# A fused attention and feed-forward kernel: who takes the first statistics, where the scaled rows come from, and how one-column matmuls are mixed with query heads

## The chip, the cores and the metric

The kernel runs on one core of a Trainium2 chip. Time is device microseconds of that core for one execution; the lower, the better. "PE" is the matmul engine (TensorE), "DVE" VectorE, "ACT" ScalarE, "SP" the engine that issues most loads. Each timed execution also reports the mean granted clock of PE as a share of full speed (1.000 is full).

## The reference, cut to what matters

```python
mod = (silu(c) @ w_mod)                        # c: 1 x 1024, w_mod: 1024 x 6144
sa, ca, ga, sb, cb, gb = ...                   # six vectors of 1024
h = layernorm(x) * (1 + ca) + sa               # x: 2048 x 1024
x = x + ga * attention(h)                      # 32 query heads of 128, 4 kv heads, last 512 keys
h = layernorm(x) * (1 + cb) + sb
x = x + gb * ffn(h)                            # 1024 -> 3584 -> 1024
```

All inputs are bf16. The attention part computes `q = h @ wq` for each of 32 heads and each of 4 blocks of 512 rows of x.

## The kernel before

Only the first phase changes. It brings in the first 512 rows of x (four tiles of 128 rows), normalises and transposes them, and computes the first seven query heads. Afterwards a long, regular sequence of steps begins (scores, exponentials, next query head, outputs). The first score matmul, written `s_ps` in the profile, marks its start; the first output matmul, `o_ps`, comes 4.34 us later in an undisturbed execution.

The trick of the first phase is this: `h = n * (1 + ca) + sa`, with `n` the normalised rows. The scaled part `hs = n * ca1` (`ca1` is `1 + ca`) can go into the query matmuls as soon as a few columns of `ca1` are known, and the part of `sa` enters as a bias per head, `bias_q = wq^T sa`. Both `ca1` and `sa` come from matmuls whose right side is a single column (`mod_cols`), and `bias_q` too (`shift_cols`).

```python
def stats_0(t):                                 # mean and variance of one tile on DVE, then
    mv = ln[t] = ...                            # 1/sqrt on ACT
    ln_stats(t, mv)
    rstd_0(t)
def act_sum(t): ...                             # the same statistics on ACT: sum, then
def act_squares(t): ...                         # squared differences (two passes)

stats_0(0); act_sum(3); stats_0(1)
xpose_0(0, ln_norm(0)); warm(4)                 # xpose_0: PE transposes into h0_ps, warm: filler matmuls
act_squares(3); stats_0(2); rstd_0(3, 1.0 / D)
xpose_0(1, ln_norm(1)); warm(4)
n2 = ln_norm(2); n3 = ln_norm(3)
mod_cols(1, 0, ca1, True, (0,))                 # first 128 values of ca1
xpose_0(2, n2); xpose_0(3, n3)
mod_cols(1, 0, ca1, True, (1, 2, 3))
# h0_ps: two PSUM tiles of [128, 4, 512] bf16; row group dt lies in h0_ps[dt // 4][:, dt % 4]
nc.scalar.activation(out=hs[0][:, 0, :], in_=h0_ps[0][:, 0, :], func=ACT.Identity, scale=ca1[:, 0:1])
nc.vector.tensor_copy(out=h10[:, 0:2, :], in_=h0_ps[0][:, 0:2, :])
h_scale(1)                                      # DVE: hs row 1 from the SBUF copy h10
nc.vector.tensor_copy(out=h10[:, 2:4, :], in_=h0_ps[0][:, 2:4, :])
h_scale(2); h_scale(3)
nc.scalar.copy(out=h10[:, 4:8, :], in_=h0_ps[1])
# ... cut ...
for dt in range(4):                             # "rounds": heads 4, 5, 6 with hs row dt
    for g in range(4, H0):
        q0(g, (dt,))
for i in range(2):                              # heads 0 to 3; their PSUM is the PSUM of h0_ps
    t = big("q_ps")
    ...
    if i == 0:
        mod_cols(1, 1, ca1, True)               # second half of ca1
# ... cut: heads 0 to 3 with rows 4 to 7 ...
sa_cols(0)                                      # 32 one-column matmuls: first half of sa
q0(4, range(4, DT))                             # 4 matmuls of 512 columns
# ... cut ...
shift_cols(0)                                   # 28 one-column matmuls: first half of bias_q
sa_cols(1)
q0(5, range(4, DT))
shift_cols(1)
q0(6, range(4, DT))
for g in range(4):
    put_q(g, q0_ps[g], bias_q[:, g:g + 1], g % 2 == 1)   # heads 0, 2 on DVE, 1, 3 on ACT
```

Nearly all loads of this phase stand in one queue, in this order: four tiles of x, then the `w_mod` blocks for `ca1` and `sa` and the first `wq` blocks in turns, then k (transposing loads), then v (four), then the `wq` blocks of heads 8 to 11.

## Time and profile before

| before | value |
|---|---|
| time | 1274.93 us, median of 3 (1273.68 to 1275.57) |
| span of the profiled execution, granted clock | 1271.9 us, 1.000 |
| first `hs` row scaled | 11.15 us |
| `mod_cols(1,1)` starts on PE | 17.17 us |
| `sa_cols(0)` starts on PE | 23.15 us |
| `bias_q` complete (starts) | 28.45 us |
| first `s_ps`, first `o_ps` | 30.24, 34.58 us |

From the profile's page of before, its first line of busy time by engine and the chain of work that ended last by engine:

```profile
PE 1262.7 (99%) x7587; PEld 641.2 (50%) x7587; DVE 609.0 (48%) x1335; ACT 334.9 (26%) x439; POOL 1.3 (0%) x10
...
PE 98%; DVE 1%; DMA 0%; issue 0%; ACT 0%; ACTq 0%
```

PE is busy nearly all the time, and it is the chain. Of the 9.2 us that PE does not fill, 3.8 lie in the first 30 us and 5.2 in the last 6 (from 1266 us, where the last outputs are stored, which the change does not touch); in between there are 0.2. So a change in the first phase can gain only what it takes off the start of the regular steps.

The next lines are from the timeline of before: start in us, duration in us, engine, source line, operation, output and inputs, shapes, number of instructions, and in brackets how long the engine sat idle first and what ended that.

```profile
9.65 1.00 DVE L852 TENSOR_SCALAR xn<-x,mv 128x1024 bf16<-128x1024 bf16 x2 [0.95 <-ACT mv L954]
...
11.15 0.69 ACT L996 ACTIVATE hs<-h_ps,modT 128x512 bf16<-128x512 bf16 x1 [1.11 <-PE h_ps L948]
...
12.03 0.69 DVE L998 COPY hT<-h_ps 128x1024 bf16<-128x1024 bf16 x1
12.76 0.35 DVE L993 TENSOR_SCALAR hs<-hT,modT 128x512 bf16<-128x512 bf16 x1
...
13.16 0.81 PE L1013 MATMUL q_ps<-hs,wq 128*128 128x512 bf16 x3 [0.47 <-DVE hs L993]
...
14.15 3.18 PE L1013 MATMUL q_ps<-hs,wq 128*128 128x512 bf16 x14 [0.18 <-DVE hs L993]
...
17.17 0.94 PE L773 MATMUL mod_ps<-siluc,wm 128*128 128x1 bf16 x32
...
23.15 0.94 PE L773 MATMUL mod_ps<-siluc,wm 128*128 128x1 bf16 x32
...
25.91 0.94 PE L773 MATMUL mod_ps<-siluc,wm 128*128 128x1 bf16 x32 [0.26 <-DVE bias_q L1027]
...
28.45 0.17 DVE L1029 TENSOR_TENSOR bias_q<-sh_ps,bias_q 128x7 f32<-128x7 f32 x1 [1.20 <-PE sh_ps L1024]
...
30.24 0.59 PE L1153 MATMUL s_ps<-qT,kT 128*128 128x512 bf16 x2
```

Three waits can be read here. DVE waits 0.95 us for ACT's statistics before the last two normalisations. PE waits 0.47 us for `hs` row 1, because DVE first copies 1024 elements a partition out of PSUM (0.69) and scales the copy after that. PE waits 0.26 us for `bias_q` before the second `sa_cols`.

### The profile page before, as it was taken

The numbers are of one execution on the slowest core, as the hardware profiler recorded it, in microseconds if no ns is written. First come the engines' busy times: TensorE is split into PE (matmuls) and PEld (weight loads), VectorE is DVE, ScalarE is ACT, GpSimd is POOL, SyncE is SP. The second block draws the span as 40 slices with busy tenths as digits, with TensorE's granted clock in tenths as the row PEclk, the third lists the DMA queues.
The fourth block names the chain that finished last, engine by engine and source line by source line (L and its number), as shares of the span: only waits on it lengthen the run. The fifth ranks groups of instructions, "written<-read, shape, count | busy, mean of one in ns | idle before, by whom it ended". The sixth has DMA issues, their size and how long they took to land.

```text
span 1271.9 us, 18166 instructions
## 1 busy us (share of the span) xinstructions
PE 1262.7 (99%) x7587; PEld 641.2 (50%) x7587; DVE 609.0 (48%) x1335; ACT 334.9 (26%) x439; POOL 1.3 (0%) x10
## 2 busy tenths in 40 slices
PE   8999999999999999999999999999999999999998
PEld 4555555555555555555554444444444444444444
DVE  4766568977587756476664632311222112221122
ACT  3543334443343433334341111011100111011100
POOL 0000000000000000000000000000000000000000
PEclk9999999999999999999999999999999999999999
DMA  9897657768556655455575466536633565425701
GB/s 290 203 246 180 175 133 176 170 171 195 142 134 173 152 137 153 113 154 112 120 203 145 135 224 184 161 96 212 210 116 102 171 213 179 157 91 172 242 22 64
DMA packets 306844, 204.46 MB, mean 161 GB/s; under 512 B 145601, under 2 KB 303297, under 8 KB 306754
## 3 DMA queue, kind: packets, MB, share of 16 engines
q1 hardware_dynamic: 301842, 199.03, 57.7%
q10 hardware_dynamic: 4912, 4.20, 1.0%
q8 instruction: 61, 1.00, 0.3%
q14 instruction: 29, 0.24, 0.1%
HBM read 165.94 MB, written 4.21 MB: 134 GB/s over the span
## 4 chain that ended last, share of the span: by engine, by line
PE 98%; DVE 1%; DMA 0%; issue 0%; ACT 0%; ACTq 0%
PE gu_ps L1299 30%; PE a_ps L1217 17%; PE q_ps L1142 16%; PE d_ps L1319 15%; PE o_ps L1185 9%; PE s_ps L1153 9%; PE q_ps L1013 1%; DVE st L833 0%; DVE junk L1076 0%; PE mod_ps L773 0%; DMA x<-in_A_x_dram 0%; PE h_ps L948 0%; DVE qT L934 0%; DVE hT L873 0%; DVE junk L804 0%
## 5 line engine op out<-in xcount | busy, mean ns | idle before, releaser
L1155 ACT ACTIVATE pT<-s_ps 128x1024 bf16<-128x1024 f32 x256 | 249.2, 1021 | 346.8 <-PE s_ps L1153 346.8
L1217 PE MATMUL a_ps<-wo,oT 128*128 128x512 bf16 x1024 | 241.9, 379 | 0.0
L1142 PE MATMUL q_ps<-hT,wq 128*128 128x512 bf16 x968 | 229.2, 379 | 0.0
L1305 DVE TENSOR_TENSOR guT<-gu_ps,sg 128x512 bf16<-128x512 f32 x112 | 77.4, 692 | 284.4 <-ACT sg L1304 284.4
L1299 PE MATMUL gu_ps<-hT,wg 128*128 128x512 bf16 x896 | 211.7, 379 | 0.0
L1304 ACT ACTIVATE sg<-gu_ps 128x512 bf16<-128x512 f32 x112 | 66.9, 597 | 488.6 <-PE gu_ps L1299 480.1
L1319 PE MATMUL d_ps<-wd,guT 128*128 128x512 bf16 (+2 forms) x952 | 194.2, 366 | 0.0
L1299 PE MATMUL gu_ps<-hT,wu 128*128 128x512 bf16 x672 | 163.3, 379 | 0.0
L1217 PEld LDWEIGHTS <-oT 128*128 128x128 bf16 x1024 | 100.2, 98 | 120.6
L934 DVE CAST qT<-q_ps 128x512 bf16<-128x512 f32 x121 | 83.6, 691 | 147.9 <-PE q_ps L1142 147.6
L1142 PEld LDWEIGHTS <-wq 128*128 128x128 bf16 x968 | 94.7, 98 | 114.1
L1319 PEld LDWEIGHTS <-guT 128*128 128x128 bf16 x952 | 90.9, 98 | 103.0
L1185 PEld LDWEIGHTS <-pT 128*128 128x128 bf16 x2048 | 126.7, 98 | 30.8 <-issue 0.4
L1299 PEld LDWEIGHTS <-wg 128*128 128x128 bf16 x896 | 87.6, 98 | 105.5
L1185 PE MATMUL o_ps<-v_sb,pT 128*128 128x130 bf16 x2048 | 137.1, 220 | 0.1
L1153 PE MATMUL s_ps<-qT,kT 128*128 128x512 bf16 x512 | 131.9, 379 | 0.1
L1299 PEld LDWEIGHTS <-wu 128*128 128x128 bf16 x672 | 65.8, 98 | 79.3
L1172 DVE TENSOR_TENSOR oq<-o_ps,rl 128x256 bf16<-128x256 f32 (+2 forms) x256 | 100.5, 419 | 3.7
L1323 DVE TENSOR_TENSOR f<-d_ps,gb_bc 128x512 f32<-128x512 f32 (+2 forms) x34 | 22.5, 660 | 140.5 <-PE d_ps L1319 140.5
L1225 DVE TENSOR_TENSOR acc<-a_ps,acc 128x512 f32<-128x512 f32 x64 | 44.1, 689 | 37.2 <-PE a_ps L1217 37.2
L1153 PEld LDWEIGHTS <-kT 128*128 128x128 bf16 x512 | 44.9, 98 | 30.8 <-issue 0.5
L1299 PE MATMUL gu_ps<-hT,v_sb 128*128 128x512 bf16 x224 | 57.5, 379 | 0.0
(92 smaller groups left out, 420.7 us busy)
## 6 DMA issues: line engine op xcount, KB each, us to landing
wq<-in_A_wq_dram SPq DMA_DIRECT2D x64, 512.0 KB
wo<-in_A_wo_dram SPq DMA_DIRECT2D x64, 512.0 KB
wg<-in_B_w_gate_dram SPq DMA_DIRECT2D x56, 512.0 KB
wd<-in_B_w_down_dram SPq DMA_DIRECT2D x56, 512.0 KB
wu<-in_B_w_up_dram SPq DMA_DIRECT2D x42, 512.0 KB
v_sb<-in_B_w_up_dram SPq DMA_DIRECT2D x14, 512.0 KB
x<-in_A_x_dram SPq DMA_DIRECT2D x16, 256.0 KB
wm<-in_w_mod_dram SPq DMA_DIRECT2D x4, 1024.0 KB
```

The lines of the kernel that those rows point to most:

```text
L934: nc.vector.tensor_copy(out=t, in_=q_ps)
L1142: nc.tensor.matmul(q_ps, lhsT=w, rhs=hT[("h1", cc)][:, dt, :], start=(dt == 0), stop=(dt == DT - 1))
L1153: nc.tensor.matmul(s_ps[:, i, :], lhsT=kT[:, kv, j * P:(j + 1) * P], rhs=qT[g], start=True, stop=True)
L1155: nc.scalar.activation(out=p[:, 2 * jj:2 * jj + 2, :], in_=s_ps, func=ACT.Exp, scale=scale)
L1172: nc.vector.tensor_tensor(out=dst, in0=ps[:, s0:s0 + cnt, 0:Dh], in1=sc, op=ALU.mult)
L1185: nc.tensor.matmul(o_slot["ps"][:, s_, :], lhsT=pT[g][:, j, t * P:(t + 1) * P], rhs=v_sb[:, kv, j, 0:VN], start=(j == 0), stop=(j == WT - 1))
L1217: nc.tensor.matmul(a_ps, lhsT=oT[(cc, 2 * q + i)][:, hh % 4, t * P:(t + 1) * P], rhs=wo_tiles[(cc, q, dh, i)][:, hh % 4, :], start=(hh == ...
L1225: nc.vector.tensor_tensor(out=acc[(cc, t)][:, dsl], in0=a_ps, in1=acc[(cc, t)][:, dsl], op=ALU.add)
L1299: nc.tensor.matmul(ps[:, n, :], lhsT=gu_w[(cc, fg, nm, dt // 4)][:, dt % 4, fi * P:(fi + 1) * P], rhs=hT[("h2", cc)][:, dt, :], start=(dt ...
L1304: nc.scalar.activation(out=g, in_=ps[:, 0, :], func=ACT.Silu)
L1305: nc.vector.tensor_tensor(out=guT[(cc, fg)][:, fi, :], in0=ps[:, 1, :], in1=g, op=ALU.mult)
L1319: nc.tensor.matmul(d_ps, lhsT=guT[(cc, f // 4)][:, f % 4, t * P:(t + 1) * P], rhs=wd_tiles[(cc, dh, f // 4)][:, f % 4, c0:c0 + w], start=( ...
```

## The change

The intent, read from the diff: ACT takes the statistics of the second tile of x instead of the fourth, so that the last normalisations need not wait for ACT. The scaled rows `hs` 0 to 3 come straight from PSUM, rows 0 and 2 on DVE, rows 1 and 3 on ACT, and the plain copies come afterwards. In the tail, one-column matmul groups and query heads of 512 columns strictly alternate.

```diff
--- before.py
+++ after.py
@@ -956,7 +956,6 @@
     def stats_0(t):
         mv = ln[t] = sm.tile([P, 4], FP32, name="mv", tag="mv", bufs=4)
         ln_stats(t, mv)
-        rstd_0(t)
 
     def act_sum(t):
         mv = ln[t] = sm.tile([P, 4], FP32, name="mv", tag="mv", bufs=4)
@@ -971,35 +970,42 @@
                              accum_out=mv[:, 1:2])
 
     stats_0(0)
-    act_sum(3)
-    stats_0(1)
+    act_sum(1)
+    rstd_0(0)
+    stats_0(2)
+    act_squares(1)
+    warm(3)
     xpose_0(0, ln_norm(0))
-    warm(4)
-    act_squares(3)
-    stats_0(2)
-    rstd_0(3, 1.0 / D)
+    rstd_0(1, 1.0 / D)
+    rstd_0(2)
+    warm(5)
+    stats_0(3)
     xpose_0(1, ln_norm(1))
-    warm(4)
-    n2 = ln_norm(2)
+    xpose_0(2, ln_norm(2))
+    rstd_0(3)
     n3 = ln_norm(3)
     mod_cols(1, 0, ca1, True, (0,))
-    xpose_0(2, n2)
     xpose_0(3, n3)
-    mod_cols(1, 0, ca1, True, (1, 2, 3))
     hT[("h1", 0)] = h10
     hs = [blkA("hs", [P, 4, TCW]) for _ in range(DH)]
 
-    def h_scale(dt):
-        nc.vector.tensor_scalar(out=hs[dt // 4][:, dt % 4, :], in0=h10[:, dt, :],
-                                scalar1=ca1[:, dt:dt + 1], scalar2=None, op0=ALU.mult)
-
-    nc.scalar.activation(out=hs[0][:, 0, :], in_=h0_ps[0][:, 0, :], func=ACT.Identity,
-                         scale=ca1[:, 0:1])
-    nc.vector.tensor_copy(out=h10[:, 0:2, :], in_=h0_ps[0][:, 0:2, :])
-    h_scale(1)
-    nc.vector.tensor_copy(out=h10[:, 2:4, :], in_=h0_ps[0][:, 2:4, :])
-    h_scale(2)
-    h_scale(3)
+    def h_scale(dt, src=None, on_act=False):
+        src = h10[:, dt, :] if src is None else src
+        if on_act:
+            nc.scalar.activation(out=hs[dt // 4][:, dt % 4, :], in_=src, func=ACT.Identity,
+                                 scale=ca1[:, dt:dt + 1])
+        else:
+            nc.vector.tensor_scalar(out=hs[dt // 4][:, dt % 4, :], in0=src,
+                                    scalar1=ca1[:, dt:dt + 1], scalar2=None, op0=ALU.mult)
+
+    h_scale(0, h0_ps[0][:, 0, :])
+    mod_cols(1, 0, ca1, True, (1,))
+    h_scale(1, h0_ps[0][:, 1, :], True)
+    mod_cols(1, 0, ca1, True, (2, 3))
+    h_scale(2, h0_ps[0][:, 2, :])
+    h_scale(3, h0_ps[0][:, 3, :], True)
+    for dt in (0, 2):
+        nc.vector.tensor_copy(out=h10[:, dt:dt + 2, :], in_=h0_ps[0][:, dt:dt + 2, :])
     nc.scalar.copy(out=h10[:, 4:8, :], in_=h0_ps[1])
 
     q0_mm = [mm("q_ps") for _ in range(H0 - 4)]
@@ -1052,10 +1058,10 @@
     for dt in range(4):
         ln_mod(("h1", 0), dt, ca1, sa)
     shift_cols(0)
+    q0(5, range(4, DT))
     sa_cols(1)
-    q0(5, range(4, DT))
+    q0(6, range(4, DT))
     shift_cols(1)
-    q0(6, range(4, DT))
     for g in range(4):
         put_q(g, q0_ps[g], bias_q[:, g:g + 1], g % 2 == 1)
     for dt in range(4, DT):
```

On every engine the order of instructions after the first phase is the same in both kernels.

## The prediction

> **What bounds it now.** The page gives PE 1262.7 of 1271.9 us busy and the chain that ended last is 98% PE. The list of waits shows no PE wait of note after 30 us; all the PE idle that can be won lies in the first 30 us (windows: PE 4.35 of 5 us busy in 10 to 15, 4.74 in 25 to 30). So the change can only move the start of the steady attention steps, the first s_ps matmul, now at 30.24 us (timeline); the rest shifts with it, its order on every engine being the same.
>
> **Statistics.** Now VectorE does x0, x1, x2 and ScalarE x3; the last two normalisations wait 0.95 for ScalarE, to 9.65. After: ScalarE does x1 (sum 1.06, square 1.15), VectorE x0, x2, x3. x0 arrives at 3.5, x3 at 6.26; x2 then at about 5.4 (estimate, interpolated), so VectorE waits about 0.4 there, and the first normalisation moves later, 6.36 to about 6.8. But the four end at about 10.1 instead of 10.65. Last transposes about 10.3 to 10.8.
>
> **Scaled rows.** Now the first four q rounds start at 11.89, 13.16, 14.15: the hs rows wait for 0.69 us copies out of PSUM first. After: hs 0 and 2 on VectorE straight from PSUM, 1 and 3 on ScalarE (0.69 each, as the one at 11.15 was). VectorE from PSUM, 512 bf16: estimate 0.42 us, from the 0.69 of a 1024-wide bf16 PSUM copy against 0.69 of a 512-wide fp32 one[...]. Rounds then start about 11.4, 12.05, 12.7, 13.35 without holes over 0.1; PE at the third round is 1.4 us earlier (12.7 against 14.15). The 1024-wide copies move behind hs and are done about 13.5, before PE needs that PSUM buffer at 14.0.
>
> **Loads.** Summing the GB/s of half-microsecond windows, plus the 0.6 us from last byte to use seen for x0 and x3: second wq block at 12.3 (needed 12.7), second gate half 15.1 (15.7), first shift half 20.9 (21.7), second 23.9 (24.9). All in time.
>
> **Alternation.** q0(5) now sits between shift_cols(0) and sa_cols(1): it hides the 0.26 us wait for bias_q. But q0(6) (0.86 us) now stands before shift_cols(1), on the chain shift_cols(1), bias_q, q of head 0, q of head 1, first s_ps (1.8 us from bias_q to s_ps, unchanged), instead of filling PE during it. From the start of sa_cols(0) to bias_q: now 5.3 us, after about 5.75. So this part gives back 0.4 to 0.5; PE will idle about 1 us in two pieces between shift_cols(1) and the first s_ps.
>
> **Sum.** sa_cols(0) about 1.45 earlier; alternation -0.45; first s_ps about 29.2, 1.0 us earlier. Time 1274.93 - 1.0 = 1273.9 us, range 1272.4 to 1275.2 (runs of one kernel spread by 1.9). Faster by over 2%: 0.005; same: 0.985; slower: 0.01.
>
> **Right or wrong is seen by:** first hs near 10.65 and q rounds without holes; VectorE hs from PSUM 0.4, not 0.7; sa_cols(0) start near 21.7 (23.15 before); no PE wait for bias_q after shift_cols(0), but idle before q_ps of head 7 and before the first s_ps; first s_ps near 29.2; total shift equal to that shift.
>
> **Would make it wrong:** a weight block landing later than estimated, PE then waiting on DMA near 12.7 or 15.7 (loses up to 0.5); VectorE reading PSUM at 0.7 us (loses about 0.25); later steps catching the shift on a DMA that keeps its absolute time.

1.45 us earlier less the 0.45 of the alternation gives the 1.0 us forecast, and the estimate of 0.42 us rests on two measured durations of before, 0.69 us each (the 1024-wide copy at 12.03 and the 512-wide fp32 one at 34.78).

## The result, and the profile after

A ratio below is the mean time of one kernel's fast runs over that of the other's fast runs of the same rounds, so it is not quite the ratio of the medians. Every kernel that was run several times stayed within 1.5% of its fastest run, and all its runs count as fast; where one run is given, it is a single timing that carries little weight, and its profile is read for intervals.

| | before | after |
|---|---|---|
| time, 6 runs each | 1275.01 us (1273.68 to 1277.67) | 1274.70 us (1273.86 to 1278.30) |
| ratio to before | | 0.9999, 95% interval 0.9984 to 1.0014 |
| span, clock of the profiled execution | 1271.9 us, 1.000 | 1272.0 us, 0.999 |
| first `hs` row | 11.15 us | 11.25 us |
| `mod_cols(1,1)` | 17.17 us | 16.88 us |
| `sa_cols(0)` | 23.15 us | 22.86 us |
| `bias_q` | 28.45 us | 28.63 us |
| first `s_ps`, first `o_ps` | 30.24, 34.58 us | 30.41, 34.75 us |

The time fell into the predicted range. That was luck in good part: the range (1272.4 to 1275.2) also holds before's own medians of 1274.93 and 1275.01, so a change that gains nothing falls into it as well. The first `s_ps`, however, came 0.17 us later, where 1.0 us earlier was predicted. All of the expected microsecond went. The page of after, the same two lines:

```profile
PE 1255.3 (99%) x7445; PEld 641.1 (50%) x7587; DVE 608.9 (48%) x1335; ACT 335.3 (26%) x440; POOL 1.3 (0%) x10
...
PE 97%; DVE 1%; issue 1%; DMA 0%; ACT 0%; SPq 0%; ACTq 0%
```

PE shows fewer matmuls (7445) than weight loads (7587) because some matmul records are missing from this trace; that is not a change of the work. The timeline of after:

```profile
5.83 1.28 DVE L833 BATCH_NORM_STATS2 st<-x 128x6 f32<-128x512 bf16 x2 [0.70 <-DMA x<-in_A_x_dram]
...
9.12 1.42 DVE L852 TENSOR_SCALAR xn<-x,mv 128x1024 bf16<-128x1024 bf16 x3
...
10.60 0.34 PE L773 MATMUL mod_ps<-siluc,wm 128*128 128x1 bf16 x8
...
11.25 0.48 DVE L998 TENSOR_SCALAR hs<-h_ps,modT 128x512 bf16<-128x512 bf16 x1
...
11.83 0.69 ACT L995 ACTIVATE hs<-h_ps,modT 128x512 bf16<-128x512 bf16 x1 [2.07 <-DVE modT L776]
...
12.55 0.48 DVE L998 TENSOR_SCALAR hs<-h_ps,modT 128x512 bf16<-128x512 bf16 x1 [0.36 <-ACT hs L995]
...
13.07 0.69 ACT L995 ACTIVATE hs<-h_ps,modT 128x512 bf16<-128x512 bf16 x1 [0.55 <-DVE hs L998]
...
13.79 1.29 DVE L1008 COPY hT<-h_ps 128x1024 bf16<-128x1024 bf16 x2 [0.75 <-ACT hs L995]
...
15.14 1.90 PE L1019 MATMUL q_ps<-hs,wq 128*128 128x512 bf16 x8 [0.46 <-DVE hT L1008]
...
16.88 0.94 PE L773 MATMUL mod_ps<-siluc,wm 128*128 128x1 bf16 x32
...
22.86 0.94 PE L773 MATMUL mod_ps<-siluc,wm 128*128 128x1 bf16 x32
...
28.63 0.17 DVE L1035 TENSOR_TENSOR bias_q<-sh_ps,bias_q 128x7 f32<-128x7 f32 x1 [1.20 <-PE sh_ps L1030]
...
28.85 1.02 PE L1148 MATMUL q_ps<-hT,wq 128*128 128x512 bf16 x4 [0.26 <-DVE bias_q L1035]
...
30.41 0.59 PE L1159 MATMUL s_ps<-qT,kT 128*128 128x512 bf16 x2 [0.54 <-ACT qT L936]
```

Read it against before. The 0.95 us wait of DVE for ACT is gone, but DVE now waits 0.70 us for the third tile of x to land. The scaled rows do come straight from PSUM, but the two engines take turns: row 2 on DVE waits 0.36 us for row 1 on ACT, row 3 on ACT 0.55 for row 2 on DVE, the copies on DVE 0.75 for row 3 on ACT. The copies therefore end at 15.08, and PE waits 0.46 us for them, since heads 0 and 1 reuse that PSUM. From `sa_cols(0)` to `bias_q` it now takes 28.63 - 22.86 = 5.77 us, where it took 28.45 - 23.15 = 5.30.

My first theory was thus: the rows lost their gain to the turns of the two engines, the statistics theirs to the landing of x, and the tail gave back 0.47 us. The rivals: the turns come from the shared SBUF output rather than the shared PSUM input; or the loads limit the phase, whatever the engines do; or gains are taken back after the first `s_ps`.

### The profile page after: what moved, and what is told of

It reads as the page before. It is cut to its first block, busy times and chain, and to the rows that moved or that the text cites. A ratio compares the mean times of both kernels' runs of the same rounds, so it can differ in the third digit from the quotient of the medians.

```text
span 1272.0 us, 18026 instructions
## 1 busy us (share of the span) xinstructions
PE 1255.3 (99%) x7445; PEld 641.1 (50%) x7587; DVE 608.9 (48%) x1335; ACT 335.3 (26%) x440; POOL 1.3 (0%) x10
## 4 chain that ended last, share of the span: by engine, by line
PE 97%; DVE 1%; issue 1%; DMA 0%; ACT 0%; SPq 0%; ACTq 0%
PE gu_ps L1305 30%; PE a_ps L1223 17%; PE q_ps L1148 16%; PE d_ps L1325 15%; PE o_ps L1191 9%; PE s_ps L1159 8%; PE q_ps L1019 1%; DMA x<-in_A_x_dram 0%; DVE junk L1082 0%; PE mod_ps L773 0%; DVE st L833 0%; ACT hs L995 0%; PE sh_ps L1030 0%; PE h_ps L948 0%; DVE hT L1008 0%
```

## The experiments

Twelve kernels were run; all gave correct results. Before was timed again next to each group of them. Because each profile is one execution and the landing of x moves by over 1 us from one to the next (DVE starts on the third tile between 5.39 us in e5 and 6.54 in e12), I compare intervals between events inside an execution rather than their absolute times. Two serve throughout: from `mod_cols(1,0)` (its first eight matmuls on PE) to `mod_cols(1,1)`, called the row interval, and from `sa_cols(0)` to `bias_q`, called the tail interval.

| kernel | DVE starts on the third x tile (landing) | row interval | tail interval | first `s_ps` | `s_ps` to `o_ps` |
|---|---|---|---|---|---|
| before | (no wait for it) | 7.09 (includes 8 transposes more) | 5.30 | 30.24 | 4.34 |
| after | 5.83 | 6.28 | 5.77 | 30.41 | 4.34 |
| e1 old tail order | 5.46 | 6.28 | 5.38 | 29.66 | 4.79 |
| e2 rows by engine | 6.28 | 5.78 | 5.77 | 30.38 | 4.74 |
| e3 rows on DVE | 5.48 | 5.76 | 5.77 | 30.15 | 5.38 |
| e5 rows by engine, old tail order | 5.39 | 5.79 | 5.44 | 31.34 (half clock) | 4.42 |
| e7 after again | 5.57 | 6.27 | 5.77 | 30.14 | 6.02 |
| e9 after, wq ahead | 6.00 | 6.27 | 5.77 | 30.59 | 4.34 |
| e12 rows by engine, wq ahead | 6.54 | 5.78 | 5.77 | 31.95 (half clock) | 4.34 |

The two intervals repeat to 0.03 us within a group, where no load is waited for, so differences of 0.5 are plain.

### e1: the old order in the tail

```diff
 shift_cols(0)
-q0(5, range(4, DT))
 sa_cols(1)
-q0(6, range(4, DT))
+q0(5, range(4, DT))
 shift_cols(1)
+q0(6, range(4, DT))
```

> After, with the order of the q heads and one-column matmuls at the end of the phase put back as before (sa_cols(1), q0(5), shift_cols(1), q0(6)); all else as after. My theory: from the start of sa_cols(0) to bias_q falls from 5.77 us (after) to about 5.3 (before had 5.30), so the first s_ps comes at about 29.95 us instead of 30.41; the 0.26 us wait of the one-column matmuls for bias_q comes back, the PE wait before the first s_ps shrinks from 0.54 to under 0.1. Rival (the order does not matter, the loss lies in the loads or the rows): first s_ps stays at 30.4.

Time 1273.51 us (one run). Lines of its timeline:

```profile
22.50 0.94 PE L773 MATMUL mod_ps<-siluc,wm 128*128 128x1 bf16 x32
...
25.32 0.95 PE L773 MATMUL mod_ps<-siluc,wm 128*128 128x1 bf16 x32 [0.31 <-DMA wm<-in_w_mod_dram]
...
27.88 0.17 DVE L1035 TENSOR_TENSOR bias_q<-sh_ps,bias_q 128x7 f32<-128x7 f32 x1 [1.20 <-PE sh_ps L1030]
...
29.66 0.59 PE L1159 MATMUL s_ps<-qT,kT 128*128 128x512 bf16 x2
```

The tail interval fell to 5.38, and the PE wait before `s_ps` vanished. So the order of the tail does cost after 0.4 to 0.5 us in this chain, as predicted. The wait in front of the second `sa_cols` is not the one for `bias_q` that I expected, but one of 0.31 us for the last `w_mod` block: this execution was early enough to meet the load. The first `s_ps` is earlier than expected (29.66 against 29.95) because x landed 0.37 us sooner.

### e2: one PSUM tile for each engine

```diff
-h0_ps[dt // 4][:, dt % 4, t * P:(t + 1) * P]      # transposes: rows 0-3 | rows 4-7
+h0_ps[dt % 2][:, dt // 2, t * P:(t + 1) * P]      # even rows | odd rows
-h_scale(1, h0_ps[0][:, 1, :], True)
+h_scale(1, h0_ps[1][:, 0, :], True)
 (rows 2, 3 and the copies accordingly; hs still goes to one shared SBUF tile)
```

> After, with the transposed rows dealt to the two PSUM tiles by parity, so that VectorE reads one tile only and ScalarE the other; the scaled rows still go to one shared SBUF tile. My theory (the two engines wait for each other because they read the same PSUM tile): the waits of hs row 2 for ScalarE (0.36), of row 3 for VectorE (0.55) and of the copies for ScalarE (0.75) vanish; heads 0 and 1 start at about 14.5 us instead of 15.14, first s_ps at about 29.8 instead of 30.41. Rival A (the shared SBUF destination tile makes them wait): waits stay, 30.4. Rival B (the second wq block lands late and PE waits for it): rounds of rows 2 and 3 do not move, 30.4.

Time 1274.97 us (one run).

```profile
11.06 0.34 PE L773 MATMUL mod_ps<-siluc,wm 128*128 128x1 bf16 x8
...
11.85 0.48 DVE L998 TENSOR_SCALAR hs<-h_ps,modT 128x512 bf16<-128x512 bf16 x1 [0.26 <-PE h_ps L948]
12.39 4.61 PE L1019 MATMUL q_ps<-hs,wq 128*128 128x512 bf16 x20
12.44 1.26 ACT L995 ACTIVATE hs<-h_ps,modT 128x512 bf16<-128x512 bf16 x2 [2.21 <-DVE modT L776]
12.68 0.48 DVE L998 TENSOR_SCALAR hs<-h_ps,modT 128x512 bf16<-128x512 bf16 x1
...
16.84 0.94 PE L773 MATMUL mod_ps<-siluc,wm 128*128 128x1 bf16 x32
```

All three turns are gone: ACT's two rows run back to back, DVE's second row overlaps them, and PE's 20 matmuls run without a hole (after shows 0.46 us in front of its last 8). The row interval is 5.78 against 6.28. The shared SBUF output remained, so rival A falls: the shared PSUM tile made the engines take turns. The gain is 0.50 rather than the expected 0.64, because the first row now waits 0.26 us for a later transpose of its tile. The first `s_ps` hardly moved (30.38) since x landed at 6.28, 0.45 later than in after: the expectation of 29.8 missed for that reason.

The turns go by the tile, not by the row: in after, row 2 on DVE waited 0.36 us for row 1 on ACT, though both only read the tile, and different rows of it.

### e3: all four rows on DVE

```diff
-h_scale(1, h0_ps[0][:, 1, :], True)
+h_scale(1, h0_ps[0][:, 1, :])
-h_scale(3, h0_ps[0][:, 3, :], True)
+h_scale(3, h0_ps[0][:, 3, :])
```

> After, with all four scaled rows taken by VectorE from PSUM, ScalarE none. My theory: no handing over, rows of 0.48 us back to back: row 3 done at about 13.4 (13.76 in after), copies done at about 14.75, heads 0 and 1 at about 14.75 instead of 15.14, first s_ps about 30.0. So one engine alone beats two that wait for each other. Rival (two engines in parallel are the gain, one engine is slower): heads 0 and 1 later than 15.14.

Time 1274.60 us (one run). The two ends of the row interval:

```profile
10.86 0.35 PE L773 MATMUL mod_ps<-siluc,wm 128*128 128x1 bf16 x8 [0.44 <-DMA wm<-in_w_mod_dram]
...
16.62 0.94 PE L773 MATMUL mod_ps<-siluc,wm 128*128 128x1 bf16 x32
```

The row interval is 5.76, as good as two engines with a tile each, and 0.5 better than two engines with one tile. The second engine was not merely useless in after; it cost half a microsecond. The first `s_ps` (30.15) missed the expected 30.0 because PE waited 0.44 us for the first `w_mod` block at 10.86.

### e4: the statistics part alone, in before

The edit is the statistics hunk of the diff, applied to before; rows and tail stay.

> Before, with only the statistics part of the change (ScalarE takes the second tile, order of normalisations, warm matmuls as after). My theory: VectorE waits about 0.7 us for the third x tile (5.83), so the last normalisation ends at about 10.5 against 10.65 before and the first s_ps moves by less than 0.2 us (30.1 to 30.35). Rival (the statistics part is a real gain and the rest of the change eats it): first s_ps at 29.7 or sooner.

Time 1275.32 us (one run).

```profile
5.57 1.29 DVE L833 BATCH_NORM_STATS2 st<-x 128x6 f32<-128x512 bf16 x2 [0.33 <-DMA x<-in_A_x_dram]
...
8.87 1.42 DVE L852 TENSOR_SCALAR xn<-x,mv 128x1024 bf16<-128x1024 bf16 x3
...
10.52 0.27 PEld L773 LDWEIGHTS <-wm 128*128 128x128 bf16 x8 [0.19 <-DMA wm<-in_w_mod_dram]
...
11.18 0.69 ACT L997 ACTIVATE hs<-h_ps,modT 128x512 bf16<-128x512 bf16 x1 [1.66 <-PE h_ps L948]
```

DVE waited 0.33 us for the third x tile (5.57). The first `hs` row came at 11.18, against 11.15 in before, `sa_cols(0)` at 23.16 against 23.15. So the statistics part gained nothing in this pair of executions, and no gain of the rival's size (0.5 us) shows. The theory fits only in part, though: the normalisations did end 0.36 us sooner than in before (10.29 against 10.65), and part of that went into a wait of 0.19 us for the first `w_mod` block, a load. One pair can't say more, since before depends on x as well, by another tile: in e11, which is before with a later load moved, the fourth tile was in use at 7.06 instead of 6.26, and the first `hs` row came at 11.94. The change thus trades a wait for the fourth tile for one for the third; what that is worth on average was not measured. The first `s_ps` came at 31.51, outside both expectations, for a reason that I had not thought of: from 28.5 to 31.9 the granted PE clock was 0.50. More on that below.

### e5: both repairs

> After with both repairs: rows dealt to two PSUM tiles by engine, and the old order of q heads and one-column matmuls. My theory, in intervals that do not depend on when x lands: from the first hs row to mod_cols(1,1) 5.0 us (after 5.63, before from its first row 6.02), from sa_cols(0) to bias_q 5.3 to 5.4 (after 5.77), so first s_ps about 1.1 us sooner than after when x and weights land alike: 29.3, or up to 0.5 later where PE waits for the last w_mod block. Time about 1.0 us under after, which 5 rounds may or may not tell from 0. Rival (gains in this phase are taken back later): first s_ps sooner, but the span from the first s_ps to the end longer than the 1241.6 to 1243.2 of the runs so far.

Median 1274.04 us (1273.39 to 1276.02, 6 runs), ratio to before 0.9985 (0.9973 to 0.9998). The row interval is 5.79, the tail interval 5.44 (0.38 of it a wait for the last `w_mod` block). But PE also waited 0.64 us for a `wq` block at 19.7, and the clock was 0.50 from 28.1 to 31.5, so the profiled first `s_ps` is at 31.34, a miss by 2 us. From the first `s_ps` to the end it took 1241.7 us, no longer than before, so the rival does not show here. Against after in the same rounds (e7, median 1274.97) e5's median is 0.93 us lower, as expected, but the runs of the two overlap.

### e6: both shift halves in one group

```diff
+sa_cols(1)
+q0(5, range(4, DT))
-shift_cols(0) ... shift_cols(1)      # 28 + 28 one-column matmuls, two bias steps
+shift_cols()                         # 56 one-column matmuls, one bias step
+q0(6, range(4, DT))
```

(with the rows of e2)

> As e2, with sa_cols(1) moved up right behind q0(4) and both shift halves in one group of 56 one-column matmuls after q0(5), one bias copy in place of copy and add. Arithmetic: sa_cols(0) to bias_q 4.9 us if the last w_mod block is there (against 5.77 and 5.30). But that block was waited for at 25.3 in e1, and sa_cols(1) would here want it at about 23.9: I expect a PE wait for DMA of 0.5 to 1.4 us there, and then first s_ps 29.2 to 29.9, no better than e5. If the block lands in time: 28.9.

Median 1274.56 us (1273.21 to 1276.79, 6 runs), ratio 0.9991 (0.9978 to 1.0005). PE waited 0.85 us in front of the second `sa_cols` (25.14) and first `s_ps` came at 30.18. The wait is put down to DVE there; the weight load just before it is put down to the `w_mod` block (1.3 us), and e1, e5 and e10 met that block at 25.3 to 25.7, so the load is the likelier one. No better than e5, as expected, though later than the 29.2 to 29.9 that I gave.

### e7: after again

> After unchanged, a control: same chip and rounds as e5 and e6, and a second profile. The third x tile lands somewhere between 5.4 and 6.3; the intervals stay within 0.1 of the first profile (first hs row to mod_cols(1,1) 5.63, sa_cols(0) to bias_q 5.77, the waits 0.36, 0.55 and 0.75 of the two engines for each other). Time within 0.2% of before.

Median 1274.97 us (1274.06 to 1276.42, 6 runs), ratio 0.9991 (0.9978 to 1.0003). The intervals repeat (6.27, 5.77; waits of 0.36, 0.55, 0.75). x landed at 5.57 and the first `s_ps` came at 30.14. Then something new:

```profile
30.14 0.59 PE L1159 MATMUL s_ps<-qT,kT 128*128 128x512 bf16 x2 [0.54 <-ACT qT L936]
...
33.89 0.60 PE L1148 MATMUL q_ps<-hT,wq 128*128 128x512 bf16 x2 [1.43 <-DMA wq<-in_A_wq_dram]
...
36.16 1.07 PE L1191 MATMUL o_ps<-v_sb,pT 128*128 128x130 bf16 x16
```

PE waited 1.43 us for the `wq` blocks of head 8, so an execution whose first `s_ps` was 0.27 us earlier than after's had its first `o_ps` 1.41 us later. The same wait, smaller, stands in e1, e2, e3, e6 and e8, in e2 and e3 partly as a wait of the weight load. From the first `o_ps` to the end all fourteen profiles take 1237.2 to 1238.0 us (span less the start of the first `o_ps`), so nothing later gives or takes: the first 37 us decide. A gain in the first `s_ps` is thus worth what the landing of these blocks leaves of it.

### e8: x in another order

```diff
-for tt in range(QT):                 # load x 0, 1, 2, 3
+for tt in (0, 2, 1, 3):
-act_sum(1); rstd_0(0); stats_0(2); act_squares(1)
+rstd_0(0); act_sum(1); stats_0(2); rstd_0(2); act_squares(1)
-xpose_0(1, ln_norm(1)); xpose_0(2, ln_norm(2))
+xpose_0(2, ln_norm(2)); xpose_0(1, ln_norm(1))
```

> After, with x loaded in the order 0, 2, 1, 3, the first rstd ahead of ScalarE's sum, the third tile normalised before the second. My theory (the statistics part gains nothing because VectorE waits for the third x tile): VectorE starts the second statistics at about 5.0 without a wait, the last normalisation ends at about 10.0 to 10.1 instead of 10.54, first hs row at about 10.7 instead of 11.25; but then PE meets the landing of the first gate weights (10.2 to 10.9 in e1 and e3) and waits for DMA, so not all of it arrives. Rival (the landing of x does not matter): first hs row stays at 10.9 to 11.8.

Time 1274.49 us (one run). DVE started the second statistics at 4.96 without a wait, as expected; the last normalisations ran from 9.24 to 10.24, 0.3 us sooner than in after, and the first row came at 10.94 instead of 11.25, not at the 10.7 that I expected: they now waited 0.55 us for ACT, which got its tile later. PE met no late block in front of the rows here. So part of the loss of the statistics part is the landing of x, and the repair moves the wait to ACT. At the end, PE waited 0.46 us for head 8's `wq` at 32.9, and the first `o_ps` came at 35.20, later than in after.

### e9, e10, e11: head 8's weights ahead of v

```diff
+load_wq(0, 2)
 for kv in range(Hkv):
     load(v_sb[:, kv, :, 0:Dh], v_v[:, kv])
-load_wq(0, 2)
```

e9 does this to after, e10 to e5, e11 to before.

> After, with the load of head 8's wq blocks issued ahead of the four v loads instead of behind them. In e7 PE waited 1.43 us for these blocks at 32.4 to 33.9, in e1, e3, e6, e8 0.2 to 1.3. Theory now: the span is the first o_ps plus a constant (1237.2 to 1238.0 in ten profiles), and the first o_ps is set by the later of PE's own work and the landing of these blocks. Expected: no PE wait for wq between 31 and 36 us, first o_ps 4.3 us after the first s_ps (34.5 to 34.8 us), unless v now lands late; time 0 to 1 us under e7's. Rival (the waits at 32 us are an artefact of the profiled run or belong to another load): waits stay, or move to v_sb with the same size.

> e5 (rows by engine, old order) with the wq load ahead of v. If the loads were what took e5's gain back: first s_ps 29.0 to 29.7, no wait for wq, first o_ps 33.5 to 34.1 in an execution with full clock, span about 1271; time 1.5 to 2.5 us under before's median of the same rounds. If a burst of clock 0.5 as in e4 and e5 (1.5 us) falls in the profile, read the intervals, not the span.

> Before, with only the wq load ahead of v: a control. If the landing of wq also costs before in some executions, its time falls by 0.3 to 1 us and the slow side of its runs (1277) thins out; in the profile the first s_ps stays at 30.0 to 30.4 and the first o_ps at 34.4 to 34.7. If wq never delays before, no difference at all.

| | median us | ratio to before of the same rounds |
|---|---|---|
| e9 (5 runs) | 1274.19 (1273.32 to 1274.78) | 0.9985 (0.9972 to 0.9998) |
| e10 (6 runs) | 1274.29 (1272.95 to 1276.09) | 0.9986 (0.9974 to 0.9998) |
| e11 (6 runs) | 1275.67 (1273.66 to 1277.81) | 1.0000 (0.9985 to 1.0015) |

e9's timeline:

```profile
30.59 0.59 PE L1159 MATMUL s_ps<-qT,kT 128*128 128x512 bf16 x2 [0.54 <-ACT qT L936]
...
34.93 1.07 PE L1191 MATMUL o_ps<-v_sb,pT 128*128 128x130 bf16 x16
```

No wait for head 8's `wq` is left in e9, e10 and e11, and from `s_ps` to `o_ps` it takes 4.34 us in e9 and e11, as in an undisturbed before; v still came in time. So the wait at 32 us was that load, and its place in the queue cures it. In before it gained nothing in the mean (e11): the profile of before had no such wait to cure, and its slow runs have another cause, as follows. The absolute times that I expected were missed where x landed late: e9's first `o_ps` came at 34.93 (expected 34.5 to 34.8; third tile at 6.00), e11's first `s_ps` and `o_ps` at 31.02 and 35.36 (expected 30.0 to 30.4 and 34.4 to 34.7; fourth tile at 7.06).

e10's profiled span was 1274.3 us, not the 1271 I hoped for, and its first `s_ps` came at 32.39, not at 29.0 to 29.7. The windows of one microsecond of e10 (PE, weight load, DVE, ACT, GpSimd busy with their instruction counts, then granted PE clock, DMA share, GB/s):

```profile
25.00:26.00 1.00, 0.64 (x26) 0.56 (x24) 0.57 (x3) 0.00 (x0) 0.00 (x0) 1.00 0.79 150
26.00:27.00 1.00, 1.00 (x30) 0.72 (x27) 0.22 (x2) 0.00 (x0) 0.00 (x0) 0.58 2.58 264
27.00:28.00 1.00, 1.00 (x4) 0.41 (x3) 0.11 (x1) 0.00 (x0) 0.00 (x0) 0.50 0.31 8
...
32.00:33.00 1.00, 1.00 (x4) 0.42 (x3) 1.00 (x3) 0.00 (x0) 0.00 (x0) 0.51 1.35 224
33.00:34.00 1.00, 1.00 (x7) 0.41 (x5) 1.00 (x2) 0.68 (x1) 0.00 (x0) 1.00 0.95 149
```

From 26.2 to 33.0 PE ran at half clock. The matmuls themselves show it; these are two query heads of e10, the same work ahead of the step and inside it:

```profile
23.67 1.02 PE L1019 MATMUL q_ps<-hs,wq 128*128 128x512 bf16 x4
...
26.57 1.87 PE L1019 MATMUL q_ps<-hs,wq 128*128 128x512 bf16 x4
```

Quarter-microsecond windows give the length as 6.8 us here, and 3.4 us in e4 (28.5 to 31.9) and in e5 (28.1 to 31.5). The granted clock in them is 0.50. This happened while PE counted as busy: for 3.04 of the 3.4 us ahead of e10's step (a stretch as long as the steps of e4 and e5). In that stretch (22.8 to 26.2) PE did one `sa_cols` (0.8 us by start times), one query head (0.86), one `shift_cols` (about 0.7), waited (0.36 in the profile's count) and began the next `sa_cols`: only about a quarter of the time went into matmuls of 512 columns, the rest into one-column ones and the wait. With the order of after there are 0.86 us of wide matmuls between any two one-column groups, and by the start times of its profile (an estimate) wide matmuls take at least 40% of every stretch of 3.4 us there. A poor stretch does not always end in a step: the profiles of before, e1 and e11 have no step there, though before's poorest stretch, 24.8 to 28.2, holds no more than a quarter either; what decides it was not shown. That stretches of mostly one-column matmuls bring on the step is thus my inference from where the steps fall, not shown by itself.

The timed runs fit. The profiled execution of e10, with a step of 6.8 us, has a mean clock of 0.996; those of e4 and e5, with 3.4 us, have 0.998. Only the lower mark is a good one: e12's profile, below, has 0.998 from a step near its start, and in the profiles of after, e1, e4 and e5 the clock is 0.50 for the last 2 to 3 us too, where PE has nothing left to do (after from 1269.1 us; its last matmul ends at 1266.8), which costs nothing and lowers the mean all the same. By these marks:

| runs with a recorded clock | number | at 0.996 | at 0.998 |
|---|---|---|---|
| before | 32 | 14 | 7 |
| e1, e4, e5, e10, e11 (old tail order) | 20 | 5 | 4 |
| e6 (56 one-column matmuls in one group) | 6 | 2 | 1 |
| after, e2, e3, e7, e8, e9 (new tail order) | 20 | 0 | 1 |

### e12: the rows by engine, the weights ahead, the new tail order

It differs from e10 by the tail order alone.

> e10 with the changed order of q heads and one-column matmuls put back in: it differs from e10 by that order alone. Theory added after e10: in executions with the old order the granted clock falls to 0.50 for about 3.4 or 6.8 us after the stretch of one-column matmuls (profiles of e4, e5, e10), which costs 1.7 or 3.4 us; so far 13 of 23 timed runs of before, 1 of 6 of e5, 2 of 6 of e10, 2 of 6 of e11 and 2 of 6 of e6 show a mean clock of 0.996, and none of 20 runs of the six kernels with the changed order. Expected: all 6 runs at 0.998 or more, most at 0.999 to 1.000, while before in the same rounds shows 0.996 in about half; in the profile no clock under 1.0 between 20 and 36 us, sa_cols(0) to bias_q 5.77, first hs row to mod_cols(1,1) 5.0, no PE wait for wq, median 1273.5 to 1274.3. Rival (the bursts come by chance, whatever the order): 2 or 3 of 6 runs at 0.996 to 0.998, as in e10.

Median 1273.84 us (1273.15 to 1275.33, 5 runs), ratio to before 0.9986 (0.9972 to 1.0000). Clocks: 0.998, 1.000, 0.999, 1.000, 0.999; no run at 0.996, where e10 had 2 of 6. Before, in the same rounds, had one of 9 at 0.996 and four at 0.998, fewer than half of the strong kind, so that part of the expectation missed. The row and tail intervals and the absence of the `wq` wait came out as expected. The profile has full clock from 20 to 36 us, but a step of 0.50 from 8.65 to 12.06: x landed at 6.54 in that execution, and PE sat idle for 2.07 us before its first transposes. This step begins 0.1 us after the end of that idle time, and 15.7 us ahead of the tail (`sa_cols(0)` at 24.39), so the changed order of the tail has no part in it.

## Why the prediction was right or wrong

The predicted time (1273.9 us, 1272.4 to 1275.2) held the measured median 1274.70, and "same" was right. But the hit is luck as far as the mechanism goes: the gain of 1.0 us did not come (first `s_ps` 0.17 us later instead), and the range was wide enough to hold a gain of nothing. Behind it, two terms were mis-sized or missing.

1. "sa_cols(0) about 1.45 earlier": measured 0.29 in the first profile and 0.56 in e7. This is the step that failed. Of the missing 1.16 us, 0.60 lie before the first row and 0.56 after it. Its first half, the first row at 10.65, came at 11.25; 0.43 of that is the third x tile, in use at 5.83, not at the interpolated 5.4 (in e7 it was in use 0.26 sooner and the first row came 0.26 sooner), and the other 0.17 was not traced. Over the profiles that tile ranges from 5.39 to 6.54. Its second half, "without holes over 0.1", overlooked that the two engines share one PSUM tile. e2 and e3 put this part at 0.50 us.

2. "alternation -0.45": right as a chain. 5.77 against 5.30 us, with PE idle 0.26 and 0.54 us, as described; e1 undid it. But it was taken as the whole meaning of the order, and a second effect was missed: with the old order, many executions have a mean clock of 0.996 or 0.998 (in the profiles of e4, e5 and e10 by a stretch at 0.50) and are slower. In the 11 runs of before, of all rounds with recorded clocks, at 0.999 or 1.000 the mean is 1274.64 us, in its 7 at 0.998 it is 1275.59 and in its 14 at 0.996 it is 1277.46, so a loss of 1.0 to 2.8 us. The 11 runs of after and e7 at 0.999 or 1.000 have 1274.79. So with full clock the two kernels are the same within the spread of their runs (+0.15 us, in line with the +0.17 of the first `s_ps`), and what differs is the slow executions: after and e7 had none at 0.996 and one at 0.998. In the first comparison few of before's runs were slow (one of six over 1277), so nothing showed; next to e7 before had 6 of 11 runs at 0.996 and its median was 1276.91 against 1274.97.

3. "VectorE from PSUM, 512 bf16: estimate 0.42": measured 0.48. The two equal durations it was taken from leave the constant part of a copy open, so 0.42 could not be more than a guess at it.

4. "All in time" of the loads: true in the profile of after, not in others. e3 waited 0.44 us for the first gate weights, e1, e5 and e10 0.31 to 0.38 for the last ones, e5 0.64 for a `wq` block. And head 8's `wq` was not on my list at all. It was covered only by the last clause, "later steps catching the shift on a DMA that keeps its absolute time", and that is what e7 shows with 1.43 us.

5. "Total shift equal to that shift": right. First `s_ps` +0.17, first `o_ps` +0.17, span +0.1.

What stays open: the half clock is tied to the tail order by its place and the counts, but e12 against e10, the one pair with several runs each that differs by the order alone, has too few to prove it by itself (2 of 6 at 0.996 against 0 of 5), and no run varied the load on PE in that stretch deliberately. Among the kernels with the new statistics and rows by two engines or one, those with the old order have 3 of 13 runs at 0.996 (e1, e5, e10) and those with the new order 0 of 25; by my count chance alone would do that in some 3% of cases. In before the share is higher (14 of 32), and whether the rest of the change has a part in that is not known. One run of after at 1278.30 us with clock 0.998 has no profile, and its cause is unknown. Whether e12 beats after can't be told from these times; e9 and e12 are 0.15% under before, with intervals that end at or just under 1, in rounds where six of eleven (e9) and one of nine (e12) of before's runs stood at 0.996.

## What to carry to other kernels

In this program two engines that read one PSUM tile took turns, even on different parts of it (0.36, 0.55 and 0.75 us): give each engine its own tile, or let one do the work. Before counting a gain at the start of a kernel, list every load that PE will meet up to the first steady step, for a gain ends where the next one lands (e7's first `s_ps` was 0.27 us earlier than after's, and PE then waited 1.43 us for `wq`). And a busy PE in the profile need not mean full clock; here half clock (0.50 for 3.4 us in e4 and e5, for 6.8 in e10) followed stretches of mostly one-column matmuls: look at the granted clock of single microseconds and of each run, not at the mean, and try mixing wide matmuls in between, which the counts of runs here favour but do not prove.
